# Linear attention block on one core: order of the last state products, of the state matmuls and the normaliser, and pieces of the last row tile

## The chip, the cores and the metric

The kernel runs on one core of one Trainium2 chip. The metric is the device time of one execution in microseconds (us), median of three runs. Further, one execution was profiled; times of single instructions come from there.

Names of engines: PE is the matrix engine (PEld its weight loads), DVE the vector engine, ACT the activation engine, POOL the general engine, SP the one that only issues transfers (DMAs).

## The reference

Input `x` is 2048 rows of 640, `wqkv` 640 by 1920, `wo` 640 by 640, all bf16. There are 32 heads of 20 columns.

```python
qkv = (x @ wqkv).reshape(B, S, 3, H, Dh).transpose(2, 0, 3, 1, 4)
q, k, v = qkv[0], qkv[1], qkv[2]
phi = lambda t: jnp.where(t > 0, t + 1, jnp.exp(t)) + 1e-6
pq, pk = phi(q), phi(k)
kv  = einsum("bhsd,bhse->bhde", pk, v)      # one 20x20 state per head
z   = einsum("bhsd->bhd", pk)               # its normaliser
num = einsum("bhqd,bhde->bhqe", pq, kv)
den = einsum("bhqd,bhd->bhq", pq, z)[..., None] + 1e-6
out = (num / den).transpose(0, 2, 1, 3).reshape(B, S, D) @ wo
```

## The kernel before, in words

Nothing of v is computed row by row. The kernel uses that the state is pk^T (x wv) = (pk^T x) wv, and that the state and `wo` can be multiplied into one matrix. Its steps:

1. **k** (lines 273 to 298): for each of 16 row tiles of 128 rows, x times wk, 640 columns as two halves of 320 in two of the eight PSUM banks; ACT's exponential and two DVE steps turn them into `pk`.
2. **State products** (`p_step`, line 303): pt = x^T pk, summed over all 16 row tiles in banks 0 to 4 (one for each 128 columns of x), first for the left half of pk's columns, then for the right half. `p_out` (line 312) copies the five banks out, ACT banks 0, 2 and 4, DVE banks 1 and 3.
3. **q tiles** (`q_tile`, line 325): 20 tiles of 128 columns by 512 rows. Five matmuls, ACT's exponential, a DVE minimum-and-add (line 341) and a DVE maximum-and-add (line 344) give `pq`. They are spread among the state products and the steps below; their banks go round in the list `small`, taken by `take`.
4. **Normaliser**: z is summed by DVE in steps among the others (`z_steps`, `z_finish`). `den` (line 448) multiplies it with pq for half the rows (1024) at a time; ACT takes the logarithm and the exponential of its negative (`den_act`), which is 1/den; `den_spread` issues broadcasts on SP's queue into `rd`, two for each 512 rows. `normalize` (line 476) multiplies a tile of pq with it on DVE, five tiles for each 512 rows.
5. **State and fold**: `kv_group` (line 401) multiplies wv with pt for six groups of six heads (the last has two), 20 matmuls into bank 0 and 10 into bank 1; `kv_mask` (line 418) keeps the 20x20 blocks of the diagonal, three DVE instructions, into `kvt`. `w2_group` (line 429) multiplies a group with its rows of wo: two matmuls of 320 columns into two banks, one copy by ACT into `w2g`. `w2_rows` (line 440) is a DMA on SP's queue that puts the rows into the order in which pq has its columns, `w2p`. All six must have landed before the first output.
6. **Output** (`out_tile`, line 515): for each of 16 row tiles, pq times w2p in two halves of 320 columns, five matmuls each; ACT copies the left half, DVE the right one, and SP issues the DMA to `out`. The last row tile (`out_last`, line 522) goes in three pieces, the last of which leaves by ACT's queue.

The order on each engine is the order in which the code calls these helpers; the class `Plan` (line 18) derives the waits. Each engine works off its own list in that order, so an instruction that waits holds all that stand behind it on its engine.

Around the change, the calls at lines 589 to 617 give this order on PE: state products of the right half with a q tile here and there, a q tile, `den` for the first 1024 rows, `kv_group`, and then six times a q tile (but for group 4) and a fold group, then four q tiles, then the outputs. With group 1 the five normalises of the first 512 rows are put into the list `todo`, and each later `next_q` takes one from it. Fold groups use banks 2 and 3 for even g, banks 0 and 1 for odd g. SP's queue gets two broadcasts, the six row transfers, and two broadcasts more.

Of the kernel before, what the change touches and what calls it, by code (L numbers as in the profile page):

```python
# [82 lines left out]
def bass_standalone__linear_attn_block__prompt_kernel(nc, x, wqkv, wo, out):  # L83
    B, S, D = x.shape
    assert (B, S, D) == (1, 2048, 640)
    H, DH = 32, 20
    NC_ = D // 128
    NT = S // 128
    HALF = D // 2
# [5 lines left out]
    with contextlib.ExitStack() as ctx:  # L95
# [205 lines left out]
        def p_step(h, st, ds=range(NC_)):  # L301

            def mm(e):
                for d in ds:
                    r = e.matmul(  # L305
                        bank(d, HALF), xn[:, st * D + 128 * d:st * D + 128 * d + 128],
                        pk[:, st * D + HALF * h:st * D + HALF * (h + 1)],
                        start=(st == 0), stop=(st == NT - 1))
                return r
            P.add("pe", mm, reads=xn_keys(st) + [("pk", st)],  # L310
                  writes=[("bank", d) for d in ds])

        def p_out(h):
            for d in range(NC_):
                dst = pt[:, d * D + HALF * h:d * D + HALF * (h + 1)]
                if d % 2 == 0:
                    P.add("act", lambda e, d=d, dst=dst: e.copy(dst, bank(d, HALF)),
                          reads=[("bank", d)], writes=[("pt", d, h)])
                else:
                    P.add("dve", lambda e, d=d, dst=dst: e.tensor_copy(dst, bank(d, HALF)),  # L320
                          reads=[("bank", d)], writes=[("pt", d, h)])

        nq = [0]

        def q_tile(sbk, c, b):
            i = nq[0] % 3
            nq[0] += 1

            def mm(e):
                for d in range(NC_):  # L330
                    r = e.matmul(  # L331
                        bank(b), wqp[:, d * D + 128 * c:d * D + 128 * c + 128],
                        xT[:, d * S + BK * sbk:d * S + BK * (sbk + 1)],
                        start=(d == 0), stop=(d == NC_ - 1))
                return r
            P.add("pe", mm, reads=[("wqp", d) for d in range(NC_)]
                  + xT_keys(BK * sbk, BK * (sbk + 1)), writes=[("bank", b)])
            t = eq[i]
            P.add("act", lambda e: e.activation(t[:, :], bank(b), ACTF.Exp),  # L339
                  reads=[("bank", b), "table"], writes=[("eq", i)])  # L340
            P.add("dve", lambda e: e.tensor_scalar(  # L341
                t[:, :], t[:, :], 1.0, 1e-6, ALU.min, ALU.add),
                reads=[("eq", i)], writes=[("eq", i)])
            P.add("dve", lambda e: e.scalar_tensor_tensor(  # L344
                pq[:, c * S + BK * sbk:c * S + BK * (sbk + 1)], bank(b), 0.0, t[:, :],
                ALU.max, ALU.add),
                reads=[("bank", b), ("eq", i)], writes=[("pq", sbk, c)])
# [53 lines left out]
        def kv_group(b):  # L401

            for lo, hi, bb in ((0, 4, b), (4, 6, b + 1)):
                def mm(e, lo=lo, hi=hi, bb=bb):
                    for g in range(lo, hi):
                        n = gsz[g]
                        for d in range(NC_):
                            r = e.matmul(  # L408
                                bank(bb, n, off=128 * (g - lo)),
                                wv[:, d * D + GW * g:d * D + GW * g + 128],  # L410
                                pt[:, d * D + GW * g:d * D + GW * g + n],
                                start=(d == 0), stop=(d == NC_ - 1))
                    return r
                P.add("pe", mm, reads=["wv", "wvpad"] + [("pt", d, h) for d in range(NC_)
                                                         for h in range(2)],
                      writes=[("bank", bb)])

        def kv_mask(b):
            for lo, n, bb, w in ((0, 4, b, GW), (4, 1, b + 1, GW), (5, 1, b + 1, 40)):
                src = ps[0:w, BK * bb + 128 * (lo % 4):BK * bb + 128 * (lo % 4) + 128 * n] \  # L420
                    .rearrange("p (g j) -> p g j", j=128)[:, :, 0:w]
                m = bm[0:w, 0:w].unsqueeze(1).broadcast_to([w, n, w])
                dst = kvt[0:w, GW * lo:GW * (lo + n)].rearrange(
                    "p (g j) -> p g j", j=GW)[:, :, 0:w]
                P.add("dve", lambda e, src=src, m=m, dst=dst: e.tensor_tensor(
                    dst, src, m, ALU.mult), reads=[("bank", bb), "bm"],
                    writes=[("kvt", g) for g in range(lo, lo + n)])

        def w2_group(g, b):
            n = gsz[g]  # L430
            for h in range(2):
                P.add("pe", lambda e, h=h: e.matmul(  # L432
                    bank(b + h, HALF, parts=GW), kvt[0:GW, GW * g:GW * (g + 1)],
                    wog[0:GW, g * D + HALF * h:g * D + HALF * (h + 1)], start=True, stop=True),
                    reads=[("kvt", g), "wog", "wog5"], writes=[("bank", b + h)])
            P.add("act", lambda e: e.copy(  # L436
                fold(w2g[0:n, g * D:(g + 1) * D]), two_banks(b, parts=n)),
                reads=[("bank", b), ("bank", b + 1)], writes=[("w2g", g)])

        def w2_rows(g):  # L440

            w = gsz[g] // NC_
            P.add("sp", lambda e: e.dma_start(
                w2p[24 * g:24 * g + w, :].rearrange("p (c n) -> p c n", n=D),
                w2g[0:gsz[g], g * D:(g + 1) * D]),
                reads=[("w2g", g)], writes=[("w2p", g)], dma=True)
# [48 lines left out]
        def out_dma(st, lo, hi, eng="sp"):  # L495
            j = st % 4
            P.add(eng, lambda e: e.dma_start(
                out[0, 128 * st:128 * st + 128, lo:hi], osb[j][:, lo:hi]),
                reads=[("osb", j, c) for c in range(lo // 160, hi // 160)],
                writes=[("out", st, lo)], dma=True)  # L500
            out_keys.append(("out", st, lo))

# [1 line left out]

        def out_evac(st, b, lo, hi, eng):
            j = st % 4
            keys = [("osb", j, c) for c in range(lo // 160, hi // 160)]
            if eng == "act":
                P.add("act", lambda e: e.copy(osb[j][:, lo:hi], bank(b, hi - lo)),  # L509
                      reads=[("bank", b)], writes=keys)  # L510
            else:
                P.add("dve", lambda e: e.tensor_copy(osb[j][:, lo:hi], bank(b, hi - lo)),  # L512
                      reads=[("bank", b)], writes=keys)
# [6 lines left out]
            out_dma(st, 0, D)  # L520

        def out_last(st, b):
            q = HALF // 2
            for n, (lo, hi, eng) in enumerate(((0, HALF, "act"), (HALF, HALF + q, "act"),
                                               (HALF + q, D, "dve"))):
                out_mm(st, b[n], lo, hi)
                out_evac(st, b[n], lo, hi, eng)
            out_dma(st, 0, HALF + q)
            out_dma(st, HALF + q, D, "act")


        pool_const()
# [25 lines left out]
        def take():  # L558
            small.append(small.pop(0))
            return small[-1]  # L560

        def next_q(n=1):
            q_tile(*qs.pop(0), take())
            for _ in range(n):
                if todo:
                    todo.pop(0)()
# [6 lines left out]
        def scale(i, s):  # L573
            todo.extend(lambda s=s, c=c: normalize(2 * i + s, c) for c in range(NC_))
# [12 lines left out]
        p_out(0)  # L587
        next_q()
        next_q()
        for st in range(NT):  # L590
            p_step(1, st)
            if st in (0, 2, 4, 6):
                zst.pop(0)()
            if st == 9:
                z_finish(take())
            if st in (1, 4, 7, 10, 12):
                next_q()
        assert not zst
        p_out(1)
        next_q()  # L600
        inverse(0)
        den_spread(0, (0, 1))
        kv_group(0)
        kv_mask(0)
        small[:] = [5, 6, 7, 4]
        for g in range(NG):
            if g != 4:
                next_q()
            w2_group(g, 2 * ((g + 1) % 2))
            w2_rows(g)  # L610
            if g == 1:
                scale(0, 0)
        den_spread(0, (2, 3))
        for _ in range(4):
            next_q()
        assert not todo
        scale(0, 1)
# [11 lines left out]
        for st in range(4, NT - 1):  # L629
# [1 line left out]
                if todo:  # L631
                    todo.pop(0)()
            out_tile(st, 2 * (st % 4) if st > 5 else 2 * (st % 2))
        out_last(NT - 1, (6, 7, 0))

        P.emit("pe", nc.tensor)
        P.emit("act", nc.scalar)
# [34 lines left out]
```

## Time and profile before

| what | us |
|---|---|
| median of 3 runs (100.43, 100.93, 101.52) | 100.93 |
| the profiled execution | 100.59 |
| its span, first to last instruction or transfer | 99.3 |
| PE busy | 95.8 |
| DVE busy | 67.9 |
| ACT busy | 43.3 |

The time of an execution has 1.29 us outside the span. Rows of the profile name a line of the kernel, the engine, the operation, `out<-in` by the names of the program, the shape, and the count; then busy time and the mean of one in ns; then the idle time of that engine just before, and what ended it. The chain is the sequence of work that ended last, followed back from the end: start, length, what.

### The profile page before, as it was taken

To read this page: it belongs to the slowest core of one execution; us is meant where nothing else is said; L and a number is where in the kernel's file an instruction comes from. 1 tells how busy PE (TensorE), PEld (TensorE's weight loads), DVE (VectorE), ACT (ScalarE), POOL (GpSimd) and SP (SyncE) were. 2 spreads that over 40 slices of the span, in tenths; PEclk is the share of its full clock that TensorE was granted. 3 is DMA by queue.
4 is the path that set the end of the run, shared out by engine and by line. 5 is a ranking of instruction groups with operands and counts; after the bars stand their busy time and mean duration, and the time that the engine had idled before them with its cause. 6 is when DMAs were issued, how large, how long until landed. Compare 5 with 4: busy or idle time off the path is not lost.

```text
span 99.3 us, 1767 instructions
## 1 busy us (share of the span) xinstructions
PE 95.8 (96%) x687; PEld 62.3 (63%) x693; DVE 67.9 (68%) x136; ACT 43.3 (44%) x76; POOL 3.2 (3%) x15
## 2 busy tenths in 40 slices
PE   6999999999999999999999999999999999999992
PEld 2567577777776666556567565755536677777771
DVE  0216988888888477999987335578899659763331
ACT  5008345554795222452231228389844622333321
POOL 6600000000000000000000000000000000000000
PEclk9999999999999999999999999999999999999999
DMA  2997999999999820000000000114440325342333
GB/s 47 351 194 167 185 203 145 155 303 389 363 363 226 169 54 3 0 3 0 0 7 0 0 0 0 27 35 121 136 123 0 131 63 175 139 155 109 132 132 132
DMA packets 18356, 12.26 MB, mean 123 GB/s; under 512 B 10029, under 2 KB 18349, under 8 KB 18349
## 3 DMA queue, kind: packets, MB, share of 16 engines
q1 hardware_dynamic: 17773, 11.63, 43.9%
q10 hardware_dynamic: 576, 0.53, 1.7%
q8 instruction: 5, 0.08, 0.4%
q14 instruction: 2, 0.02, 0.1%
HBM read 5.90 MB, written 2.62 MB: 86 GB/s over the span
## 4 chain that ended last, share of the span: by engine, by line
PE 81%; DMA 7%; DVE 4%; SPq 3%; ACT 2%; issue 1%
PE ps L487 22%; PE ps L305 22%; PE ps L278 17%; PE ps L331 16%; DMA xT<-in_x_dram 4%; DMA xn<-in_x_dram 3%; SPq L184 3%; DVE pq L344 2%; PE ps L408 2%; PE ps L454 1%; ACT eq L339 1%; DVE pq L479 1%; PE ps L432 1%; DVE eq L341 1%; ACT w2g L436 1%
## 5 line engine op out<-in xcount | busy, mean ns | idle before, releaser
L305 PE MATMUL ps<-pk,xn 128*128 128x320 bf16 x160 | 23.5, 299 | 0.0
L331 PE MATMUL ps<-xT,wqp 128*128 128x512 bf16 x94 | 23.1, 379 | 0.3
L278 PE MATMUL ps<-wk,xT 128*128 128x320 bf16 x160 | 22.2, 299 | 0.2
L487 PE MATMUL ps<-w2p,pq 128*128 128x320 bf16 (+1 forms) x165 | 22.1, 295 | 0.2 <-DVE pq L479 0.2
L339 ACT ACTIVATE eq<-ps 128x512 bf16<-128x512 f32 x20 | 12.0, 599 | 21.2 <-PE ps L331 20.7
L305 PEld LDWEIGHTS ps<-pk,xn 128*128 128x128 bf16 x160 | 15.6, 98 | 7.4 <-DVE pt L320 0.2
L487 PEld LDWEIGHTS ps<-w2p,pq 128*128 128x128 bf16 x165 | 15.8, 98 | 6.7 <-DVE pq L479 0.7
L278 PEld LDWEIGHTS ps<-wk,xT 128*128 128x128 bf16 x160 | 15.4, 98 | 6.9 <-DMA wk<-in_wqkv_dram 0.5
L291 ACT ACTIVATE ek<-ps 128x640 bf16<-128x640 f32 x16 | 11.2, 704 | 13.9 <-PE ps L278 13.9
L331 PEld LDWEIGHTS ps<-xT,wqp 128*128 128x128 bf16 x100 | 9.7, 97 | 9.0
L344 DVE SCALAR_TENSOR_TENSOR pq<-ps,eq 128x512 bf16<-128x512 f32 x20 | 13.8, 691 | 0.7
L296 DVE SCALAR_TENSOR_TENSOR pk<-ps,ek 128x640 bf16<-128x640 f32 x16 | 13.2, 824 | 0.6
L512 DVE CAST osb<-ps 128x320 bf16<-128x320 f32 (+1 forms) x16 | 7.7, 479 | 8.4 <-PE ps L487 7.7
L509 ACT CAST osb<-ps 128x320 bf16<-128x320 f32 (+1 forms) x17 | 7.0, 416 | 13.5 <-PE ps L487 11.5
L341 DVE TENSOR_SCALAR eq<-eq 128x512 bf16<-128x512 bf16 x20 | 5.8, 292 | 9.8 <-ACT eq L339 9.7
L293 DVE TENSOR_SCALAR ek<-ek 128x640 bf16<-128x640 bf16 x16 | 5.2, 325 | 5.1 <-ACT ek L291 5.1
L479 DVE TENSOR_TENSOR pq<-pq,rd 128x512 bf16<-128x512 bf16 x20 | 7.7, 416 | 0.5 <-DMA rd<-rdc 0.5
L350 DVE TENSOR_TENSOR za<-pk 128x1280 f32<-128x1280 bf16 x4 | 5.8, 1482 | 0.0
L350 DVE TENSOR_TENSOR za<-za 128x1280 f32<-128x1280 f32 x3 | 4.4, 1481 | 0.0
L259 ACT COPY wqp<-wqn 128x640 bf16<-128x640 bf16 x5 | 4.3, 925 | 0.0
L436 ACT CAST w2g<-ps 120x640 bf16<-120x640 f32 (+1 forms) x6 | 4.0, 690 | 0.0
L269 PE MATMUL ps<-const-bfloat16-1.0 128*128 128x512 bf16 x6 | 2.7, 623 | 0.8 <-PEq L657 0.8
(38 smaller groups left out, 29.8 us busy)
## 6 DMA issues: line engine op xcount, KB each, us to landing
out_dram<-osb SPq DMA_DIRECT2D x15, 160.0 KB, 1.8
xn<-in_x_dram SPq DMA_DIRECT2D x2, 800.0 KB, 10.8
wqn<-in_wqkv_dram SPq DMA_DIRECT2D x1, 800.0 KB, 7.1
wv<-in_wqkv_dram SPq DMA_DIRECT2D x1, 800.0 KB, 14.5
wog<-in_wo_dram SPq DMA_DIRECT2D x1, 750.0 KB, 14.4
w2p<-w2g SPq DMA_DIRECT2D x5, 150.0 KB
xn<-in_x_dram SPq DMA_DIRECT2D x1, 640.0 KB, 8.3
rd<-rdc SPq DMA_DIRECT2D x8, 64.0 KB, 2.1
```

Source lines behind the costliest of these rows:

```text
L278: r = e.matmul(bank(b + h, HALF), xT[:, c * S + 128 * st:c * S + 128 * st + 128], wk[:, c * D + HALF * h:c * D + HALF * (h + 1)], start=(c ...
L291: P.add("act", lambda e: e.activation(fold(t[:, :]), two_banks(b), ACTF.Exp), reads=banks + ["table"], writes=[("ek", st % 3)])
L296: P.add("dve", lambda e: e.scalar_tensor_tensor(fold(pk[:, st * D:(st + 1) * D]), two_banks(b), 0.0, fold(t[:, :]), ALU.max, ALU.add), rea ...
L305: r = e.matmul(bank(d, HALF), xn[:, st * D + 128 * d:st * D + 128 * d + 128], pk[:, st * D + HALF * h:st * D + HALF * (h + 1)], start=(st ...
L331: r = e.matmul(bank(b), wqp[:, d * D + 128 * c:d * D + 128 * c + 128], xT[:, d * S + BK * sbk:d * S + BK * (sbk + 1)], start=(d == 0), sto ...
L339: P.add("act", lambda e: e.activation(t[:, :], bank(b), ACTF.Exp), reads=[("bank", b), "table"], writes=[("eq", i)])
L344: P.add("dve", lambda e: e.scalar_tensor_tensor(pq[:, c * S + BK * sbk:c * S + BK * (sbk + 1)], bank(b), 0.0, t[:, :], ALU.max, ALU.add), ...
L350: P.add("dve", lambda e: e.tensor_tensor(d_ap, a, b, ALU.add), reads=ra + rb, writes=[dst])
L479: P.add("dve", lambda e: e.tensor_tensor(v, v, rd[i][:, BK * o:BK * (o + 1)], ALU.mult), reads=[("rd", i, 2 * o), ("rd", i, 2 * o + 1), (" ...
L487: r = e.matmul(bank(b, hi - lo), pq[:, c * S + 128 * st:c * S + 128 * st + 128], w2p[:, c * D + lo:c * D + hi], start=(c == 0), stop=(c == ...
L509: P.add("act", lambda e: e.copy(osb[j][:, lo:hi], bank(b, hi - lo)), reads=[("bank", b)], writes=keys)
L512: P.add("dve", lambda e: e.tensor_copy(osb[j][:, lo:hi], bank(b, hi - lo)), reads=[("bank", b)], writes=keys)
```

## The change

Three places:

- **The last state products.** Row tiles 14 and 15 of the right half are no longer multiplied one after the other with all five banks each, but bank by bank: tile 14 and 15 into bank 0, then both into bank 1, and so on.
- **State, normaliser, fold.** `kv_group` and `kv_mask` are called from inside the q tile behind the state products: on PE after its matmuls, on ACT after its exponential, on DVE ahead of its two steps. The denominator follows `kv_group` on PE. Fold group 0 follows the denominator without a q tile between, and its copy is done by DVE; the other groups keep ACT. Groups 1, 2, 4 and 5 have a q tile just ahead, group 3 follows group 2, and five q tiles, not four, are left behind the last group. The first two normalises come behind the third q tile. Bank 4 is put at the head of the list `small` instead of the list being written anew.
- **The last row tile** has four pieces: columns 0 to 319 (ACT), 320 to 479 (DVE), 480 to 575 (ACT), 576 to 639 (DVE). SP's queue sends columns 0 to 479, ACT's queue the rest, as before. The names by which the planner follows the output buffer stand for 32 columns instead of 160.

```diff
-        def q_tile(sbk, c, b):
+        def q_tile(sbk, c, b, between=None):
...
             P.add("act", lambda e: e.activation(t[:, :], bank(b), ACTF.Exp),
                   reads=[("bank", b), "table"], writes=[("eq", i)])
+            if between:
+                between()
             P.add("dve", lambda e: e.tensor_scalar(
...
-        def w2_group(g, b):
+        def w2_group(g, b, eng="act"):
...
-            P.add("act", lambda e: e.copy(
+            P.add(eng, lambda e: (e.copy if eng == "act" else e.tensor_copy)(
                 fold(w2g[0:n, g * D:(g + 1) * D]), two_banks(b, parts=n)),
                 reads=[("bank", b), ("bank", b + 1)], writes=[("w2g", g)])
+            w2_rows(g)
...
         def out_last(st, b):
-            q = HALF // 2
-            for n, (lo, hi, eng) in enumerate(((0, HALF, "act"), (HALF, HALF + q, "act"),
-                                               (HALF + q, D, "dve"))):
+            for n, (lo, hi, eng) in enumerate(((0, HALF, "act"), (HALF, 480, "dve"),
+                                               (480, 576, "act"), (576, D, "dve"))):
                 out_mm(st, b[n], lo, hi)
                 out_evac(st, b[n], lo, hi, eng)
-            out_dma(st, 0, HALF + q)
-            out_dma(st, HALF + q, D, "act")
+            out_dma(st, 0, 480)
+            out_dma(st, 480, D, "act")
...
-        for st in range(NT):
+        for st in range(NT - 2):
             p_step(1, st)
...
+        for d in range(NC_):
+            p_step(1, NT - 2, (d,))
+            p_step(1, NT - 1, (d,))
         p_out(1)
-        next_q()
+
+        def state_groups():
+            kv_group(0)
+            kv_mask(0)
+        next_q(between=state_groups)
         inverse(0)
         den_spread(0, (0, 1))
-        kv_group(0)
-        kv_mask(0)
-        small[:] = [5, 6, 7, 4]
-        for g in range(NG):
-            if g != 4:
-                next_q()
-            w2_group(g, 2 * ((g + 1) % 2))
-            w2_rows(g)
-            if g == 1:
-                scale(0, 0)
+        small.insert(0, 4)
+        w2_group(0, 2, "dve")
+        next_q()
+        w2_group(1, 0)
+        scale(0, 0)
+        next_q(2)
+        w2_group(2, 2)
+        w2_group(3, 0)
+        next_q()
+        w2_group(4, 2)
+        next_q()
+        w2_group(5, 0)
         den_spread(0, (2, 3))
-        for _ in range(4):
+        for _ in range(5):
             next_q()
...
-        out_last(NT - 1, (6, 7, 0))
+        out_last(NT - 1, (6, 7, 0, 1))
```

More of the change, by code (lines that the diff above doesn't have):

```diff
@@ L498, in out_dma @@
                 out[0, 128 * st:128 * st + 128, lo:hi], osb[j][:, lo:hi]),
-                reads=[("osb", j, c) for c in range(lo // 160, hi // 160)],
+                reads=[("osb", j, c) for c in range(lo // 32, hi // 32)],
                 writes=[("out", st, lo)], dma=True)
@@ L506, in out_evac @@
             j = st % 4
-            keys = [("osb", j, c) for c in range(lo // 160, hi // 160)]
+            keys = [("osb", j, c) for c in range(lo // 32, hi // 32)]
             if eng == "act":
@@ L560, in take, with next_q @@
             return small[-1]
-        def next_q(n=1):
-            q_tile(*qs.pop(0), take())
+        def next_q(n=1, between=None):
+            q_tile(*qs.pop(0), take(), between)
             for _ in range(n):
```

## The prediction, made before the change was run

> **What bounds the kernel now.** I read the head of the page first, then busy time by stage, then the chain that ended last.
>
> ```profile
> span 99.3 us, 1767 instructions
> PE 95.8 (96%) x687; PEld 62.3 (63%) x693; DVE 67.9 (68%) x136; ACT 43.3 (44%) x76; POOL 3.2 (3%) x15
> PEclk9999999999999999999999999999999999999999
> ```
>
> TensorE (PE) is busy for 96% of the span at full clock, so only PE's own work, its gaps, and what lies before its first and after its last matmul can move the time. The stages are cut at the start of the k products, of the state products, of the q tile behind the last state product, of the output rows, and of the last copy. Columns are length, then busy time and count for PE, PEld, DVE, ACT and POOL.
>
> ```profile
> 10.57:27.05 16.48, 16.48 (x122) 11.88 (x123) 14.12 (x26) 8.97 (x13) 0.00 (x0) 1.00 1.01 251
> 27.05:59.83 32.78, 32.62 (x217) 20.77 (x220) 24.97 (x40) 11.85 (x20) 0.00 (x0) 1.00 0.26 65
> 59.83:74.67 14.84, 14.48 (x109) 8.08 (x111) 11.39 (x27) 10.88 (x21) 0.00 (x0) 1.00 0.27 74
> 74.67:97.38 22.71, 22.67 (x185) 16.18 (x185) 13.74 (x34) 8.23 (x20) 0.00 (x0) 1.00 0.33 114
> 97.38:99.30 1.92, 0.00 (x0) 0.00 (x0) 0.32 (x1) 0.00 (x0) 0.00 (x0) 1.00 0.50 168
> ```
>
> The change works in the third stage, at the end of the second, and in the last two. PE lacks 0.36 us in the third stage. The chain (start, length, what) tells what that is.
>
> ```profile
> 59.83 0.05 issue
> 59.88 1.03 PE ps L331 x4
> 60.90 0.66 PE ps L454 x20
> 61.56 1.54 PE ps L408 x30
> ...
> 64.19 0.27 PE ps L432 x2
> 64.46 1.08 PE ps L331 x5
> ...
> 74.18 0.34 DVE pq L479
> 74.52 0.15 issue
> 74.67 2.88 PE ps L487 x20
> 77.55 0.66 PE ps L454 x20
> ...
> 97.36 0.02 issue
> 97.38 0.32 DVE osb L512
> ```
>
> A q tile has five matmuls and takes 1.08 us. At 59.83 the chain shows 0.05 of "issue" and four matmuls in 1.03: one record is missing, not a gap. Counting PE's work from 59.83, ten q tiles (10.80), the denominator (0.66), kv (1.54) and six fold groups of 0.27 (1.62) make 14.62, so PE would be through at 74.45. The first output matmul starts at 74.67. About 0.2 us is a real wait there, behind the fifth normalise, which ends at 74.52; no other PE gap of size lies in what the change touches.
>
> **The middle, part by part.** PE's work is the same there: same matmuls, same shapes, other order. So I follow whether each waits for something, from a few rows of the timeline (start, length, engine).
>
> ```profile
> 59.86 1.08 ACT L317 CAST pt<-ps 128x320 bf16<-128x320 f32 x3 [1.44 <-PE ps L305]
> 61.62 0.47 ACT L464 ACTIVATE lb<-ps,eps 128x256 f32<-128x256 f32 x1
> 62.12 0.42 ACT L466 ACTIVATE rdc<-lb 128x256 bf16<-128x256 f32 x1
> 62.76 0.94 DVE L425 TENSOR_TENSOR kvt<-ps,bm 120x480 bf16<-120x480 f32 x3 [0.17 <-PE ps L408]
> 64.72 0.69 ACT L436 CAST w2g<-ps 120x640 bf16<-120x640 f32 x1
> 65.43 6.40 SPq L443 DMA_DIRECT2D w2p<-w2g  x6
> 75.36 0.28 DVE L341 TENSOR_SCALAR eq<-eq 128x512 bf16<-128x512 bf16 x1
> 75.67 0.69 DVE L344 SCALAR_TENSOR_TENSOR pq<-ps,eq 128x512 bf16<-128x512 f32 x1
> 76.28 0.48 DVE L512 CAST osb<-ps 128x320 bf16<-128x320 f32 x1
> ```
>
> Last state products bank by bank. The last ten products of the second half (two rows, five banks) run as five pairs instead of two rows. Bank 0 is finished four pairs (eight products of 0.135 us each, half of the fold row's 0.27, which has the same 320 columns) before the last. The three ACT copies then no longer run as one block of 1.08 from 59.86 to 60.94; the last needs only about 0.36 behind 59.83 and ends near 60.25. The q tile hides either until 60.91, so this alone is worth nothing. It is needed because kv comes next; without it kv would wait some 0.05 us.
>
> State products ahead of the normaliser. kv runs 60.91 to 62.45, the denominator 62.45 to 63.11. The first mask needs 20 of the 30 kv matmuls: 61.94, plus the 0.17 of the mask row, 62.11. The three masks took 0.94, so all end by 63.05. Fold group 0, the first two matmuls after the denominator, can start at 63.11: no wait, with 0.06 to spare against the third mask and over 0.3 against the first, which it really needs. The q tile that used to be the cover here is replaced by the denominator.
>
> What became later: DVE's work on that q tile now stands behind the masks, 62.97 to 63.9 instead of 61.57 to 62.6. Nobody on PE needs its bank until the q tile of 66.35. ACT's logarithm and exponential come 1.55 later, 63.17 to 64.09, and the two broadcasts on SP's queue with them.
>
> First group copied by DVE. The trace has no such copy on DVE; the nearest rows bound it.
>
> ```profile
> L296 DVE SCALAR_TENSOR_TENSOR pk<-ps,ek 128x640 bf16<-128x640 f32 x16 | 13.2, 824 | 0.6
> L512 DVE CAST osb<-ps 128x320 bf16<-128x320 f32 x15 | 7.3, 489 | 7.6 <-PE ps L487 6.9 <-DMA out_dram<-osb 0.6
> L512 DVE CAST osb<-ps 128x160 bf16<-128x160 f32 x1 | 0.3, 324 | 0.9 <-PE ps L487 0.9
> DMA to landing us min/median/max: 2.1/2.1/2.6
> ...
> L339 ACT ACTIVATE eq<-ps 128x512 bf16<-128x512 f32 x20 | 12.0, 599 | 21.2 <-PE ps L331 20.7
> ```
>
> From 160 to 320 columns a cast grows by 0.165, so 640 gives an estimate of 0.82, which the 0.824 of the line-296 row supports; twice the 0.489 (0.98) is the upper end, ACT's 0.69 the lower. I take 0.82: 63.9 to 64.72. PE wants those two banks again for group 2, after q tile, group 1, q tile: 63.38, 64.46, 64.73, 65.81. That leaves 1.1 us. On SP's queue the copy is ready at 64.75; the two broadcasts issue from 64.11 for 1.3 us, so the first row transfer still leaves about 65.4, as before.
>
> The wait that goes. Broadcasts issued at 64.1 and 64.75 land 2.1 to 2.6 later (the row of landings), 66.9 to 67.4. Normalising starts after the third q tile: its PE work ends 65.81, its exponential, 0.06 later and 0.60 long, 66.47, its two DVE steps (about 0.3 and 0.61 start to start) 67.42. Then two normalises, and one behind each of the next three q tiles. ACT alternates exponentials (0.60, the last row above) and group copies until then; the sixth q tile's exponential follows its PE end at 70.13 and is done at 70.8. DVE takes it at 70.82, so the fifth normalise ends near 72.2, 2.3 us ahead of 74.45. The last row transfer: group 5 leaves PE at 69.05 and ACT by 69.9. In before it was issued by 71.8 at the latest (the SP row) behind a copy that ended 71.1, and had landed when PE began at 74.67, at most 3.6 after its copy; so here by 73.5. PE goes on at 74.45: gain 0.2. The bounds are 0 (another wait takes the place) and 0.22.
>
> What is late next: four q tiles now stand behind the last of these normalises. DVE's last q step ends at about 76.1, 1.7 behind the start of the outputs; in before, 76.36, 1.7 behind 74.67. The second denominator needs it at 77.2 and waits for nothing. The outputs' copies, transfers and second set of normalises all move with PE.
>
> **The tail.** The last 320 columns go as 160, 96 and 64 over two engines, instead of 160 and 160.
>
> ```profile
> 96.69 0.64 ACT L509 CAST osb<-ps 128x320 bf16<-128x320 f32 x2 [0.93 <-PE ps L487]
> 97.74 0.35 ACTq L497 DMA_DIRECT2D out_dram<-osb  x1
> ...
> out_dram<-osb SPq DMA_DIRECT2D x1, 120.0 KB, 1.7
> ...
> out_dram<-osb ACTq DMA_DIRECT2D x1, 40.0 KB, 1.5
> ...
> L394 DVE COPY zc<-ps 128x5 f32<-128x5 f32 x1 | 0.2, 164 | 0.0
> L487 PEld LDWEIGHTS ps<-w2p,pq 128*128 128x128 bf16 x165 | 15.8, 98 | 6.7 <-DVE pq L479 0.7 <-issue 0.2
> ```
>
> The span ends when ACT's 40 KB transfer lands: 97.74 + 1.5 = 99.24 of 99.3. SP's 120 KB, issued when ACT's second copy ends at 97.33, lands near 99.06. After the change the DVE cast of the last 64 columns takes 0.157 + 64 x 0.00103 = 0.22 us (the 160 and 320 rows above as a line) against 0.324; bounded by 0.164 (five columns) and 0.324, the gain is 0 to 0.16. I take 0.10. It starts at 97.38 as before: DVE's 160-column piece runs 97.05 to 97.37, just in time. ACT's 96 columns follow the matmuls of 97.22 and end before 97.55. SP's transfer starts at 97.40, 0.04 later than before, and lands by 99.1, under the 99.14 that ACT's now gives. So minus 0.10.
>
> PE's cost there: ten matmuls of 160 columns become five of 160, five of 96, five of 64, the same columns but five more weight loads. At 0.068 for 160 columns, half of the fold row's 0.135, five take 0.34. kv is the nearest row: 30 matmuls of 120 or 40 columns, each with its own load, in 1.54, or 0.051 each, which is about their columns and no more. At that pitch ten small matmuls cost at most 0.51 against 0.34 for the five they replace; by columns, 0.34. The five 40-column ones close kv without stretching it much, so I take 0, upper end 0.17. If each 0.098 load stood open, ten would cost 0.98, 0.64 more.
> The Trainium skill, "TensorE: Matmul & The Clock Gate", section "Back-to-back issue gap", gives a sustained pitch of about 81 ns for 128-column matmuls with their loads; by it the ten small ones would cost about 0.81 instead of 0.34, an estimate, and the whole change would lose 0.2 us. The trace's 51 ns at 120 columns speaks against it.
>
> **Sum.** The profiled execution took 100.59 us for its span of 99.3. 100.59 - 0.20 - 0.10 = 100.29. That execution lay 0.34 below the median of the runs, 100.93, so on their scale the forecast is 100.93 - 0.30 = 100.6. About 1% (1.0 us) is what a measurement of this kernel tells from no change: its three runs alone spread from 100.43 to 101.52.
>
> **Rivals.** (a) Nothing is gained: the first output matmul waits for the last row transfer, or for its seven semaphores (the 0.15 of "issue" behind the normalise stays), and SP's 120 KB decides the end. For: 0.15 is long for a hand-over, and the landing of those transfers is not shown. Against: 0.9 us of margin. Time 100.9.
> (b) Weight loads stand open in the small pieces: plus 0.64, minus 0.30, gives 101.3, slower than before by 0.3%. It decides from a pitch of 0.064 us (0.34 + 0.30 over ten). For: the 0.098 of a single load; against: kv's 0.051. The rule of the Trainium skill named above, from "TensorE: Matmul & The Clock Gate", points the same way, less far.
> (c) DVE becomes the bound: the moved copy and the later q tile push it behind, and the second denominator at 77.2 finds its input missing. The margin is 1.1 us and beyond it PE loses one for one; the copy at its upper end uses 0.16 of it, and late broadcasts (0.5 more than their longest) half of the rest. A DVE stretch 2.4 us longer than worked would give 101.9.
> (d) Fold group 0 waits for the masks: if the masks ran 0.5 later than worked, PE stops 0.2 to 0.5 there and the gain is eaten: 100.8.
>
> **How the numbers follow.** Forecast 62%, (a) 18%, (b) 6%, (c) 4%, (d) 5%, and 5% for what I haven't seen. All named cases lie between 100.6 and 101.9, but the spread of the runs is as large as the cases: a median of three can fall 0.5 to either side. The lower end is 100.6 less 0.6 (the bounds of the terms give another 0.08, the rest is the spread); the upper end, 101.3, takes in (a) and (b). Faster by over 1% needs a median under 99.9, which no term reaches: 0.07, for a lucky median. Slower by over 1% needs 101.9: 0.06, from (c), the unseen and the spread. Within 1%: 0.87.
>
> **What would show it.** In the profile after, PE's idle time before the first output matmul is gone and the outputs start near 74.45; the fold group's first matmuls show no wait for the masks; the DVE copy of group 0 takes 0.8; the fifth normalise ends some 2 us ahead of the outputs; the last DVE cast takes about 0.22, and the stretch from the last matmul's end to the span's end is 1.8 instead of 1.94; kv, the denominator and the tail matmuls keep their pitch. Wrong it is if a new PE wait shows in front of fold groups, of q tiles (banks) or of the second denominator, or if the last 15 small matmuls take over 0.7 us.

## The result and the profile after

| | before | after |
|---|---|---|
| median of 22 runs, us | 101.06 (100.43 to 101.69) | 100.64 (100.32 to 101.31) |
| the profiled execution, us | 100.59 | 100.64 |
| its span, us | 99.3 | 99.1 |

The ratio is 0.9961, with a 95% interval of 0.9943 to 0.9980: 0.4 us faster, by about the 0.30 that was forecast, and within 1%. The two profiled executions alone, 100.59 and 100.64, would not have told it: the one of after began its k products 0.15 us later (10.72 instead of 10.57), since a first load landed later, and had 1.54 us outside the span instead of 1.29.

So stretches are compared that begin behind the loads. "Stretch" below means the time from the q tile behind the last state product to the end of the last matmul: 59.83 to 97.36 before, **37.53 us**, and 59.98 to 97.18 after, **37.20 us**. First the busy time by stage after, cut as in the prediction (length, then busy time and count of PE, PEld, DVE, ACT and POOL):

```profile
27.20:59.98 32.78, 32.78 (x221) 20.77 (x220) 25.33 (x42) 12.70 (x22) 0.00 (x0) 1.00 0.21 57
59.98:74.64 14.66, 14.66 (x114) 8.43 (x113) 10.83 (x27) 9.51 (x17) 0.00 (x0) 1.00 0.29 75
74.64:97.20 22.56, 22.53 (x191) 16.15 (x188) 14.50 (x36) 8.34 (x20) 0.00 (x0) 1.00 0.33 114
97.20:99.10 1.90, 0.00 (x0) 0.00 (x0) 0.23 (x1) 0.10 (x1) 0.00 (x0) 1.00 0.51 169
```

PE is now busy for all of the 14.66 us ahead of the outputs, where it stood for 0.2 of the 14.84 before. The chain after (start, length, what) runs on PE without a break from there to the last copy:

```profile
59.98 1.08 PE ps L331 x5
61.05 1.43 PE ps L410 x30
62.49 0.66 PE ps L457 x20
63.15 0.41 PE ps L434 x2
...
69.25 5.40 PE ps L331 x25
74.64 2.72 PE ps L490 x20
77.36 0.66 PE ps L457 x20
78.02 19.16 PE ps L490 x150
97.18 0.02 issue
97.21 0.23 DVE osb L515
```

Three things are to be seen beside the rows of before. The wait ahead of the outputs is gone. The first 20 output matmuls take 2.72 instead of 2.88. And the state matmuls, which now follow a q tile, take 1.43 instead of 1.54, while fold group 0, which now follows the denominator, takes 0.41 instead of 0.27.

These lengths need a word. The chain counts a piece from the end of the piece before it. Measured from their own first start, the 20 output matmuls take the same time in both kernels, as the timelines of before (first) and after show:

```profile
74.67 2.88 PE L487 MATMUL ps<-w2p,pq 128*128 128x320 bf16 x20 [0.20 <-DVE pq L479]
```
```profile
74.48 2.88 PE L490 MATMUL ps<-w2p,pq 128*128 128x320 bf16 x20
```

After, the first of them starts at 74.48, 0.16 ahead of the end of the last q tile at 74.64: PE's matmuls overlap. Where PE has stopped, there is nothing to overlap with, and these 0.16 are lost on top of the idle time. Below this is called the start from standstill.

The timeline of after shows DVE's side (start, length, engine):

```profile
62.14 0.94 DVE L427 TENSOR_TENSOR kvt<-ps,bm 120x480 bf16<-120x480 f32 x3 [1.72 <-PE ps L410]
...
63.93 0.81 DVE L438 CAST w2g<-ps 120x640 bf16<-120x640 f32 x1
...
68.62 0.76 DVE L482 TENSOR_TENSOR pq<-pq,rd 128x512 bf16<-128x512 bf16 x2 [0.94 <-DMA rd<-rdc]
...
72.75 0.41 DVE L482 TENSOR_TENSOR pq<-pq,rd 128x512 bf16<-128x512 bf16 x1
...
76.17 0.69 DVE L346 SCALAR_TENSOR_TENSOR pq<-ps,eq 128x512 bf16<-128x512 f32 x1
```

The copy of group 0 is done at 64.74, ahead of group 2, which begins at 65.8. The first normalise waited until 68.62 for its broadcasts, and the fifth ends at 73.16, 1.5 us ahead of the outputs.

### The profile page after: what moved, and what is told of

The parts are those of the page before. It is cut to its first block, busy times and chain, and to the rows that moved or that the text cites. A ratio compares the mean times of both kernels' runs of the same rounds, so it can differ in the third digit from the quotient of the medians.

```text
span 99.1 us, 1786 instructions
## 1 busy us (share of the span) xinstructions
PE 95.7 (97%) x698; PEld 62.5 (63%) x698; DVE 68.4 (69%) x138; ACT 43.0 (43%) x75; POOL 3.2 (3%) x15
## 4 chain that ended last, share of the span: by engine, by line
PE 87%; DMA 7%; SPq 3%; DVE 0%; issue 0%; ACT 0%
PE ps L490 22%; PE ps L305 22%; PE ps L331 22%; PE ps L278 17%; DMA xT<-in_x_dram 4%; DMA xn<-in_x_dram 3%; SPq L184 3%; PE ps L434 2%; PE ps L410 1%; PE ps L457 1%; PE ps L392 0%; DVE osb L515 0%; ACT L229 0%
## 5 line engine op out<-in xcount | busy, mean ns | idle before, releaser
L331 PE MATMUL ps<-xT,wqp 128*128 128x512 bf16 x100 | 24.0, 379 | 0.0
L490 PE MATMUL ps<-w2p,pq 128*128 128x320 bf16 (+3 forms) x170 | 22.1, 291 | 0.0
L515 DVE CAST osb<-ps 128x320 bf16<-128x320 f32 (+2 forms) x17 | 7.9, 464 | 7.6 <-PE ps L490 7.6
L199 DVE COPY xT<-ps 128x256 bf16<-128x256 bf16 (+1 forms) x4 | 1.0, 318 | 3.5 <-PE ps L194 3.5
```

What stands on the lines that cost most here:

```text
L331: r = e.matmul(bank(b), wqp[:, d * D + 128 * c:d * D + 128 * c + 128], xT[:, d * S + BK * sbk:d * S + BK * (sbk + 1)], start=(d == 0), sto ...
L490: r = e.matmul(bank(b, hi - lo), pq[:, c * S + 128 * st:c * S + 128 * st + 128], w2p[:, c * D + lo:c * D + hi], start=(c == 0), stop=(c == ...
```

## The experiments

Twelve kernels ran. The times are ratios to the kernel before on the same chip, with their 95% intervals. Since these intervals are 0.2 to 0.4% either way, and several effects are no larger, the readings rest on the stretch. It comes from one profiled execution of each kernel, but the five kernels without a wait agree to 0.03 us (37.20 to 37.23).

| run | ratio (95%) | stretch, us |
|---|---|---|
| the whole change | 0.9961 (0.9943 to 0.9980) | 37.20 |
| e1_middle | 0.9982 (0.9961 to 1.0003) | 37.20 |
| e2_tail | 1.0009 (0.9989 to 1.0029) | 37.48 |
| e3_norm_early | 1.0008 (0.9987 to 1.0029) | 37.47 |
| e4_row_order | 1.0022 (1.0006 to 1.0038) | 37.51 |
| e5_act_copy | 0.9965 (0.9945 to 0.9985) | 37.21 |
| e6_q_between | 1.0097 (1.0069 to 1.0124) | 38.47 |
| e7_norm_late | 1.0105 (1.0065 to 1.0145) | 38.92 |
| e8_pieces64 | 0.9959 (0.9938 to 0.9980) | 37.23 |
| e9_rows_early | 1.0116 (1.0080 to 1.0152) | 38.55 |
| e10_both_early | 1.0067 (1.0042 to 1.0091) | 38.10 |
| e11_rows_late | 0.9981 (0.9957 to 1.0006) | 37.21 |
| e12_both_tail | 1.0082 (1.0056 to 1.0108) | 38.11 |

### The two halves of the change

e1_middle is the changed kernel with the old tail:

```diff
-            for n, (lo, hi, eng) in enumerate(((0, HALF, "act"), (HALF, 480, "dve"),
-                                               (480, 576, "act"), (576, D, "dve"))):
+            q = HALF // 2
+            for n, (lo, hi, eng) in enumerate(((0, HALF, "act"), (HALF, HALF + q, "act"),
+                                               (HALF + q, D, "dve"))):
...
```

> The change without its tail: the last row tile in three pieces as before. The time from the first k matmul to the last matmul (the PE stretch) was 86.79 us before (10.57 to 97.36) and 86.46 after (10.72 to 97.18). Theory 1 (the whole gain on PE is the lost wait ahead of the first output matmul, 0.20 of idle plus 0.16 that the first 20 output matmuls take longer when PE starts them from standstill, 2.88 against 2.72): PE stretch 86.46, time lower by 0.3 us. Rival (the wait alone, as the prediction sized it, and the rest from the smaller pieces of the tail): PE stretch 86.59. The end behind the last matmul stays at 1.94.

The stretch is 37.20 (the chain's record of the first q matmul is missing, so its start is taken 0.06 earlier). All of PE's gain is the middle's. The time, 0.18% lower, agrees with 0.3 us within its interval, which takes in no change as well.

e2_tail is the reverse, the kernel before with the new tail:

> The kernel before with only the last row tile in four pieces. Theory 1: PE stretch as before, 86.8; the last DVE cast 0.225 instead of 0.324; ACT's queue issues its transfer 0.28 behind the last matmul instead of 0.38; the end comes 0.1 us earlier. Rival (the landing of the last transfer varies by as much, 1.5 before and 1.6 after): the end behind the last matmul stays at 1.9 and no difference in time can be seen. Rival of the weight loads: the PE stretch grows by 0.2 to 0.6.

The stretch is 37.48; the 0.05 it lies under 37.53 is in the wait ahead of the outputs, 0.09 of "issue" on its chain instead of 0.15. The last DVE cast took 0.23 and ACT's queue issued 0.28 behind the last matmul, as expected. Yet from the last matmul to the end of the span passed 1.92 us, against 1.96 before: 0.04 of the 0.10 came through. In the runs with these four pieces (after, e2, e4 to e7, e11, e12) this end is 1.91 to 1.92; in those with three (before, e1, e3, e9, e10) 1.96 to 1.97. So it is real, and too small for the times to show it.

### What PE waited for ahead of the outputs

The prediction named the fifth normalise. e3_norm_early takes the kernel before and only moves the normalises:

```diff
             if g != 4:
-                next_q()
+                next_q(2)
```

> The kernel before with only the normalises of the first 512 rows taken earlier: two behind each q tile ahead of a fold group, so that the fifth stands behind the sixth q tile instead of the eighth. Theory 1 (the wait ahead of the outputs is the whole gain on PE): the wait goes, the first 20 output matmuls take 2.72, PE stretch 86.45, time lower by 0.3 us without any other part of the change. Rival (the new order of state products, normaliser and fold is what gains): PE stretch stays near 86.8 or falls by less than 0.1.

This theory fell. The normalises were done early, and the wait stayed. The timeline and the chain of e3:

```profile
71.74 0.41 DVE L479 TENSOR_TENSOR pq<-pq,rd 128x512 bf16<-128x512 bf16 x1
```
```profile
73.06 1.46 PE ps L331 x6
74.52 0.14 issue
74.66 2.88 PE ps L487 x20
```

The fifth normalise ends at 72.15, 2.4 us ahead, and PE still stands for 0.14 and then takes 2.88. The first output matmul waits for DVE and for the six row transfers; DVE is out, so the transfers remain. (They are followed to their landing below.) e7_norm_late tries the other direction, the changed kernel with its normalises late:

```diff
-        next_q(2)
+        next_q(0)
         w2_group(2, 2)
         w2_group(3, 0)
-        next_q()
+        next_q(0)
```

> The changed kernel with its normalises later, one behind each of the fifth to ninth q tiles, so that the fifth is done some 0.8 us behind the last q tile's matmuls. Theory 1: PE's idle time ahead of the outputs comes back, as long as that, the first 20 output matmuls take 2.88 instead of 2.72, and the PE stretch is 86.46 plus the idle time plus 0.16. Rival (the order ahead of it has made PE independent of the normalises): 86.46.

Its chain:

```profile
75.89 0.34 DVE pq L482
76.23 0.05 issue
76.27 2.89 PE ps L490 x20
```

PE's last q tile ended at 74.72 (60.06 plus the 14.66 of after), so it stood for 1.55 and then took 0.17 more for the first 20 matmuls: 1.72, which is 38.92 less 37.20. The stop was longer than the 0.8 that was expected. A wait on this path costs its idle time and 0.16 to 0.17 for starting from standstill. A real hand-over from DVE takes 0.05 here, not the 0.15 that stood behind the normalise in before.

Three runs then moved the last fold group. e9_rows_early and e10_both_early put it right behind the fifth in the kernel before, the latter with early normalises too; e12_both_tail adds the new tail. The edit of e10, where e9 keeps `next_q()`:

```diff
-            if g != 4:
-                next_q()
+            if g not in (4, 5):
+                next_q(2)
...
-        for _ in range(4):
+        for _ in range(5):
```

> The kernel before with its last fold group right behind the fifth, one q tile earlier, and five q tiles left behind it; the normalises stand behind the same q tiles as before. Measured from the start of the q tile behind the last state product to the last matmul: 37.53 before, 37.20 after, 37.47 with the normalises alone made early. Theory R (the first output matmul waits for the last row transfer, which lands 3.5 us behind its issue, and the fifth normalise comes at nearly the same time): the rows are then early, the fifth normalise still ends some 0.05 us behind the last q tile's matmuls, idle time about 0.1, stretch about 37.43. Theory W (0.15 us are what seven waits in front of one matmul cost): 37.53.

> The kernel before with both: the last fold group one q tile earlier and the normalises two behind each q tile. Theory R (row transfer and normalise bind together; only taking both away frees PE): idle time gone, the first 20 output matmuls 2.72, stretch 37.17 to 37.20, the whole gain of the change on PE without its new order of state products, normaliser and DVE copy. Theory W (the seven waits): 37.47 as with the normalises alone.

> The kernel before with the last fold group one q tile earlier, the normalises two behind each q tile, and the last row tile in four pieces; state products, denominator, state matmuls and group 0's copy stay as before. If these three edits are the whole of the change's gain: stretch 37.17 to 37.20, end behind the last matmul 1.92 instead of 1.96, time as with the whole change, 0.4 us under the kernel before. If the new order of state products and normaliser carries part of it: less.

All three lost 0.7 to 1.2%, by a wait that the expectations had missed. The timeline and the chain of e10:

```profile
68.93 1.95 ACT L436 CAST w2g<-ps 120x640 bf16<-120x640 f32 x3
69.67 0.48 PE L432 MATMUL ps<-wog,kvt 120*120 120x320 bf16 x2 [0.72 <-ACT w2g L436]
```
```profile
69.67 0.48 PE ps L432 x2
70.15 5.40 PE ps L331 x25
75.55 2.72 PE ps L487 x20
```

Groups 3, 4 and 5 stood together, and the last needs the banks that ACT had still to copy for group 3: 0.72 of idle time and 0.21 for the start (0.48 on the chain instead of 0.27). Without these 0.93, e10's stretch would be 37.17: ahead of the outputs it has no wait, and its first 20 matmuls take 2.72 on its chain. The same seven waits stand there as in before, so seven waits that are all met in time cost nothing. But e10 also started the outputs 0.9 later, which gives the transfers that time too, so it doesn't show how early they must be. In e9 the fifth normalise, later too, ended behind PE's q tiles and held it, as in e7. e12's tail ended as in the other runs with four pieces, and its middle as e10's.

e11_rows_late delays the last group in the changed kernel by one q tile, to where it stood before:

```diff
         w2_group(4, 2)
         next_q()
+        next_q()
         w2_group(5, 0)
         den_spread(0, (2, 3))
-        for _ in range(5):
+        for _ in range(4):
```

> The changed kernel with its last fold group one q tile later, so that its row transfer is issued about 11.35 us behind the last state product, as in the kernel before (11.30; 10.35 in the changed kernel). Normalises as in the changed kernel, done 2 us early. Theory R: the wait comes back, 0.15 to 0.25 idle and 0.16 for the start from standstill, stretch 37.5 to 37.6. Theory W, or a wait on the normalise alone: 37.20.

Theory R in this form fell as well: no wait, 37.21, though the last transfer was issued 11.31 us behind the last state product, as late as in before (11.30). So the issue alone doesn't decide. The landings do. Each landing raises a semaphore; no view of the profile lists these events for the row transfers, but the traces hold them, and PE's wait instructions too. Read from there, in us of each trace:

| run | last transfer issued | its last landing | first weight load of the outputs | did PE stand? |
|---|---|---|---|---|
| before | 71.13 | 74.29 | 74.64 | yes |
| e2_tail | 71.49 | 74.66 | 74.93 | yes |
| e3_norm_early | 71.19 | 74.31 | 74.63 | yes |
| e6_q_between | 72.16 | 75.78 | 76.05 | yes |
| after | 70.33 | 73.90 | 74.27 | no |
| e11_rows_late | 71.36 | 74.04 | 74.35 | no |
| e10_both_early | 71.27 | 74.42 | 75.17 | no |

In the four runs with a wait, the first weight load of the outputs comes 0.27 to 0.35 behind that landing, though in e3 and e6 the fifth normalise is 2.4 us old by then. What lies between are PE's own waits. It waits for the six transfers in three or four instructions, at most two at a time. In before they stand at 74.32, 74.43 and 74.57, the last three of e3 at 74.34, 74.45 and 74.56, and the weight load follows 0.08 behind the last. In both kernels the first of these three names the late transfer, and the other two, whose transfers had landed by 73.79, follow it, 0.11 apart but for the last of before. In e11 only one instruction stands behind the late one (74.07 and 74.18). Which transfer stands where differs from kernel to kernel: the planner sorts its waits by a number that is the same for all transfers, so their order is left to chance.

So theories R and W were each half of it: the last transfer lands late, and behind a late landing the waits still to come are worked off in turn. In before the normalise, done at 74.51, can have added no more than 0.03: the third wait comes 0.14 behind the second, not 0.11.

The landing depends on what the queue holds ahead of the transfer. SP's rows of e11 (first) and of before:

```profile
68.26 1.59 SPq L446 DMA_DIRECT2D w2p<-w2g  x2
...
71.36 0.70 SPq L446 DMA_DIRECT2D w2p<-w2g  x1
```
```profile
69.49 2.34 SPq L443 DMA_DIRECT2D w2p<-w2g  x3
```

In e11 the last transfer leaves 1.5 us behind the end of the fifth's issue, and it lands 2.68 behind its own issue. In before the last three leave without a pause, and it takes 3.16. In after and in e6 all six leave with less than 0.07 between them, and it takes 3.57 and 3.62. So the change sends its last transfer 0.95 earlier, counted from the last state product, and gets it 0.54 earlier (13.92 instead of 14.46). That is enough, but not by much: 0.37 us lie between the landing and the weight load of after, and by the runs with a wait up to 0.35 of that could have been needed. (In after it was less, since the late transfer happens to stand in the last instruction.) The two quantities, crowd and landing, go together over these runs; no run changes only the spacing in the kernel before.

### The order of the last state products

e4_row_order is the changed kernel with row order back:

```diff
-        for d in range(NC_):
-            p_step(1, NT - 2, (d,))
-            p_step(1, NT - 1, (d,))
+        p_step(1, NT - 2)
+        p_step(1, NT - 1)
```

> The changed kernel with the last two row tiles of the state products one after the other again. ACT's third copy then ends 1.08 us behind the last state product, when the q tile's matmuls end too. As the prediction had it: the state matmuls wait some 0.05 us, PE stretch 86.5. If a wait costs its idle time and another 0.15 for starting from standstill: PE stretch 86.65 to 86.7. If the q tile hides it wholly: 86.46.

Its chain:

```profile
60.05 1.03 PE ps L331 x4
61.08 0.14 issue
61.22 1.59 PE ps L410 x30
```

PE stands for 0.14 ahead of the state matmuls, and these then take 1.59 on the chain instead of 1.43: 0.30 in all, stretch 37.51. That is nearly all that the change gains on PE. So this order, which by the prediction's argument is worth nothing by itself (no run has it alone), is what lets the state matmuls come first. The time agrees in sign; it is 0.2% longer than before, where the stretches would make the two equal, and that rest is not explained.

### What follows the denominator

e6_q_between puts a q tile between the denominator and fold group 0:

```diff
-        w2_group(0, 2, "dve")
         next_q()
+        w2_group(0, 2, "dve")
         w2_group(1, 0)
```

> The changed kernel with the second q tile between the denominator and fold group 0 instead of behind that group. In the changed kernel the group's two matmuls took 0.41 on the chain instead of 0.27, and the state matmuls 1.43 instead of 1.54. Theory A (whatever stands behind the denominator pays 0.11 to 0.14, since its weights are not loaded ahead): the q tile then takes about 1.2 instead of 1.08 on the chain, the group 0.27, PE stretch 86.46. Theory B (fold group 0 waits for the masks): both take their usual time and the PE stretch falls to 86.32.

Its chain and two rows of its timeline:

```profile
62.82 0.66 PE ps L457 x20
63.48 1.20 PE ps L331 x5
...
76.00 0.09 issue
76.08 2.88 PE ps L490 x20
```
```profile
64.51 0.71 PE L434 MATMUL ps<-wog,kvt 120*120 120x320 bf16 x4
67.14 0.75 PE L434 MATMUL ps<-wog,kvt 120*120 120x320 bf16 x4 [0.84 <-DVE w2g L438]
```

Theory A holds: the q tile behind the denominator takes 1.20, and the group at its usual place has no wait. So 0.11 to 0.14 are lost by whatever follows the denominator's matmuls; in before it was the state matmuls (1.54 against 1.43). The change only moved it. The weight loads show it too, here of before and of after:

```profile
61.49 1.50 PEld L408 LDWEIGHTS ps<-pt,wv 128*128 128x128 bf16 x30 [0.21 <-issue]
```
```profile
63.07 0.18 PEld L434 LDWEIGHTS ps<-wog,kvt 120*120 120x120 bf16 x2 [0.21 <-DVE kvt L427]
```

Both first loads behind a denominator come after 0.21 of idle time. That the second is put down to a mask is therefore no sign of a wait for it: the time is the same where no mask is near. The whole stretch is not 37.20 as theory A expected, though: groups 0 and 1 now stand one q tile ahead of groups 2 and 3, DVE's copy of group 0 comes behind another q tile's steps, and group 2 waits 0.84 for its banks. With the start from standstill (groups 2 and 3 take 0.75 instead of 0.55) that is 1.04. This is the wait that the copy on DVE could have made in the change, and did not. The other 0.25 stand ahead of the outputs: 0.09 idle and 2.88 instead of 2.72, behind the last row transfer, as in the table above, with the normalises done 2.4 us before. The last row transfer is issued 11.85 behind the last state product here, and 10.35 in after.

e5_act_copy gives the copy back to ACT:

```diff
-        w2_group(0, 2, "dve")
+        w2_group(0, 2)
```

> The changed kernel with fold group 0 copied by ACT like the others. ACT would copy from about 64.1 to 64.8, behind 1/den and ahead of the second q tile's exponential. Theory 1: PE stretch stays 86.46, since the copy lies off PE's path on either engine; DVE ends its last q step up to 0.8 earlier unless the broadcasts hold it at the first normalise, as they did in the changed kernel (0.94 of idle time there). Rival (the DVE copy is needed, ACT falls behind and fold groups wait for banks): PE stretch over 86.6.

Stretch 37.21 and 0.9965: as the change. Which engine copies group 0 makes no difference here.

### The price of small pieces

e8_pieces64 cuts the right 320 columns of the last row tile into five pieces of 64, of which SP's queue sends three and ACT's queue two:

```diff
...
-((0, HALF, "act"), (HALF, 480, "dve"), (480, 576, "act"), (576, D, "dve"))
+((0, HALF, "act"), (320, 384, "dve"), (384, 448, "act"), (448, 512, "dve"),
+ (512, 576, "act"), (576, D, "dve"))
...
```

> The changed kernel with the right 320 columns of the last row tile as five pieces of 64, 25 matmuls, each with its own weight load. If matmuls cost their columns, these take 0.68 as in the changed kernel and the PE stretch stays 86.46; by kv's pitch of 0.051 at most 1.28, PE stretch 87.0; by the Trainium skill's 81 ns (TensorE: Matmul & The Clock Gate, section Back-to-back issue gap) 2.0, PE stretch 87.8; with open weight loads 2.45.

On the chain:

```profile
78.47 19.19 PE ps L490 x160
97.65 0.02 issue
```

160 matmuls take 19.19, where after's 150 took 19.16. With 0.68 for after's fifteen (320 columns at 0.135 for five), the 25 take 0.71, or 0.028 each. Weight loads do not stand open: 25 of them at 0.098 would be 2.45. The Trainium skill's pitch of 81 ns (TensorE: Matmul & The Clock Gate, section Back-to-back issue gap) is given there for 128 columns. Two narrower rows here are well below it: 0.048 over the 30 state matmuls (1.43; 25 of 120 columns and five of 40), and 0.028 at 64 columns.

## Why the prediction was right, and where its steps were off

- **Size and sign** were right: 0.30 forecast; 0.33 on PE and 0.04 at the end by the trace; 0.39% (0.2 to 0.57%) by the times. That the sum fits so well is in part luck: PE gained 0.13 more than the prediction's 0.20, and the tail 0.06 less than its 0.10. That nothing moves by 1%, because PE is full and has one gap, was right too.
- **The lost wait, "gain 0.2", with 0.22 as its upper bound**, was too small. The step counted idle time and left out the start from standstill: 0.20 of idle and that 0.16 went, and 0.03 came back (fold group 0's 0.14 more than the state matmuls' 0.11 less). Its working also set "PE would be through at 74.45", and that did come: 14.66 behind the q tile's start against 14.62.
- **"A real wait there, behind the fifth normalise"** named the wrong cause. PE waited for the last row transfer, which landed at 74.29, and then for its own remaining wait instructions, 0.35 in all; the normalise added at most 0.03. The chain named DVE's normalise, 0.15 ahead of PE's start, where a hand-over from DVE takes 0.05 in e7. The prediction saw that 0.15 and used it for rival (a) instead of doubting the name. e3 shows that with the normalise gone the wait stays. The change makes both early, the transfers and the normalise, and so the gain came nevertheless. That is luck as far as the cause goes: the same reasoning, followed alone in e3, gained 0.06.
- **The last row transfer "by 73.5", with "0.9 us of margin"**: it landed at 73.90, and the weight load that needs it came at 74.27, with PE's waits still between. Six transfers without a pause take longer than the three of before, which the working left out. The margin was 0.3 us at most.
- **"Without it kv would wait some 0.05 us"**: 0.30 (e4), 0.14 idle and 0.16 for the start from standstill.
- **Fold group 0: "no wait"** was right; the 0.41 that it takes is the denominator's, as e6 shows. The prediction did not know that part.
- **The DVE copy**: 0.82 forecast, 0.81 measured, off the path.
- **The broadcasts**: 2.1 to 2.6 to landing was taken from before. After, the longest took 3.7, so the first normalise began at 68.62 rather than 67.42, and DVE's last q step ended at 76.86 rather than 76.1. Rival (c) was nearer than it looked, but the second denominator at 77.36 still had 0.5 us.
- **The tail: "minus 0.10"** became 0.04. The last cast was 0.10 shorter, as worked out; but from ACT's issue to the end of the span passed 1.64 us instead of 1.58. With four pieces ACT's transfer is issued 0.26 behind SP's 120 KB instead of 0.39. That the two disturb each other is argued only.
- **Rivals**: (b), open weight loads, is refuted by e8. Its counter-figure, kv's 0.051, is a mean over matmuls of 120 and of 40 columns. (a) did not happen in the kernel after, but what it describes, the last row transfer and the waits in a row, is what held the kernel before, and e6 has it again. (d) did not happen.

## What to carry to other kernels

Where one matmul waits for an engine and for transfers, the engine that a profile names is only the last event that it can see. A hand-over that takes 0.15 instead of the 0.05 of its like says that something else was last; moving the named engine's work alone then gains nothing. Take away the named cause in a run of its own before building on it, and compare the landings. Where a transfer is the cause, what leaves just ahead of it on the queue counts beside its own issue (e11 issued its last transfer as late as before and did not wait). A stop of PE costs its idle time and 0.16 to 0.21 us more here, so a gap that is nearly hidden is worth more than it shows. A step that seems worth nothing alone, like the order of the last products, may be what the next step stands on; take it out of the finished version to see its price.

## What the runs showed of the hardware that was not expected

- A stop of PE costs 0.16 to 0.17 us beyond its idle time ahead of the output and the state matmuls (2.88 against 2.72 on the chain for twenty; 1.59 against 1.43 for thirty), the same for a stop of 0.14 (e4) and of 1.55 (e7). The matmuls are not slower: from their first start they take 2.88 and 1.59 without a stop too. What is lost is that the first starts ahead of the end of the matmul before it (74.48 against 74.64 in after).
- Wait instructions of PE behind one that is released late are worked off 0.11 us apart, though what they wait for is long done (74.34, 74.45 and 74.56 in e3); met in time, they cost nothing (e10).
- The last row transfer, 50 KB, landed 2.68 us behind its issue with a pause of 1.5 us ahead of it (e11), 3.16 as the third in a row (before), and 3.57 and 3.62 with all six in a row (after, e6).
- What follows the denominator's matmuls (32 weight columns at four positions) takes 0.11 to 0.14 us longer on the chain: 1.54 against 1.43 for the state matmuls, 0.41 against 0.27 for a fold group, 1.20 against 1.08 for a q tile.
- A 64 KB broadcast landed between 2.1 and 3.7 us behind its issue in one execution.
